# One adaLN transformer block on one core: moving the last modulation row out of the start, re-filling TensorE's waits there, and running one projection by column halves

## The chip, the cores and the metric

The kernel runs on one core of a Trainium2 chip. A core has a matmul engine (TensorE, PE in the profile, with its weight loads as PEld), a vector engine (DVE), a scalar engine (ACT), a general engine (POOL) and a queue engine (SP), which work side by side and wait for each other by semaphores, and 16 DMA engines that move data between HBM and on-chip memory. The metric is device time in microseconds (us) of one execution, taken as the median of several.

## The reference, cut to what matters

One sequence of 2048 tokens, width D = 576, 32 heads of 18, hidden width F = 4608. Everything is bfloat16.

```
mod = silu(c) @ w_mod                         # one row of 6*576: sa, ca, ga, sb, cb, gb
h = layernorm(x) * (1 + ca) + sa
q, k, v = h @ wqkv                            # per head, scale 18**-0.5
o[s] = softmax over 8 keys (s, s-2, ... s-14) of q[s].k, times v
x = x + ga * (o @ wo)
h = layernorm(x) * (1 + cb) + sb
x = x + gb * (((h @ w_gate) * (h @ w_up)) @ w_down)
```

So `ga` is needed when the first attention output is projected, and `gb` only when the first `w_down` product is written out.

## The kernel before, in words

The tokens go through in ten chunks (`SIZES`: four of 128, then six of 256). Each chunk has a first half, `project` (layer norm, a transposition of the rows, modulation by `sa`/`ca`, then q, k and v), and a second half, `attend` (logits from products of q with shifted k, softmax, weighted sum of shifted v, projection by `wo`, residual, second layer norm, transposition, modulation by `sb`/`cb`). The gated matmuls of a chunk are `gate_up`; `down` multiplies by `w_down` for 512 tokens at a time. There are seven passes over the gate/up weights: chunks 0, 1, 2 and 3 alone (passes 0 to 3, 128 tokens each), and then pairs of 256-token chunks. In pass p the matmuls of `gate_up` are interleaved with `attend` of the next chunk(s) and `project` of the one after; a `Pacer` releases these pieces when the pass has reached a set share of its length. The shares are the tables `AT_SHORT`, `AT_FIRST` and `AT`: `wo0=.59, v0=.66` means that the `wo` projection is issued at 59% of a pass and v at 66%. In passes 0 to 3 a scheduler orders the instructions on every engine; from pass 4 on TensorE's order is as written.

Everything before pass 0 is the prologue (lines 783 to 824): its order on all engines is as written by hand, as a list of `next(...)` and `go(..., label)` on three generators, `a0 = project(0)`, `a1 = project(1)` and `b0 = attend(0)`. `warm(n)` (L275) issues n matmuls on zeros whose result nobody reads. In the order of TensorE the prologue is:

- `warm`, the columns of `sa`/`ca` (L245, four 32-column groups of the array side by side), the transposition of chunk 0 (L414), `warm(9)`;
- q and k of chunk 0 (L485, forty matmuls `pq`), their last 64 columns (L492, five matmuls `pr` against a packed copy `wqr`), `warm(5)`, the transposition of chunk 1;
- logits of chunk 0 (L553, `lgT`), with the ten matmuls of the `ga` row (L264) between their two halves; the columns of `sb`/`cb` (L245);
- v of chunk 0 (L510, `pv`, ten matmuls), which waits for the weights `wv`; the shifted softmax weights (`up`, L587); v of chunk 1 (L510);
- the weighted sum (L603, `oTs`), `wo` of chunk 0 (L628, ten matmuls into the two banks of one tile `pw`, halves alternating), q and k of chunk 1 (L485), the ten matmuls of the `gb` row (L264), the transposition for the second layer norm (L414), and then `pgu` (L672), the first matmul of pass 0.

On DVE the projection is followed by two multiplications by `ga` (L633), one addition (L634), statistics in two halves (L377) and their merging (L378); ACT computes the reciprocal deviation (L383, L384); DVE normalises (L395); after the transposition ACT and DVE modulate (L434, L436). ACT copies the two row results into `ga_bc` and `gb_bc` (L268, L269).

Loads are put in queues by three engines. POOL's queue holds, in order: `wmB` (the `sb`/`cb` columns), `wv`, `wo`, the `gb` columns of `w_mod` (two DMAs, 576 KB and 72 KB, into the free half of `wmC`), the v rows of chunks 0 and 1 to HBM (L517), the gate/up weights of blocks 0 to 2 (`load_early`, L284), the shifted reads of v (`vsh`, L527), and blocks 3 to 6. SP's queue holds `c`, the `sa`/`ca` and `ga` columns, q/k weights, x, and the short weight tails `gr`; at the end of pass 0 (L340 to L346, after its next-to-last block) it gets x of chunks 4 and 5, part of `w_down`, and then two blocks of weights for pass 1, each held until DVE has written one element behind the hidden values of that block.

PSUM, where TensorE writes, is divided into two pools: `att` (two banks) and `mlp` (three tiles of two banks). `banks2` and `bank` choose between them. The v projection of a chunk (`pvA`, `pvB`) takes the two `att` banks that `wo` (`pwA`, `pwB`) had just before.

## Time and profile before

| | |
|---|---|
| runs | 5: median 578.23 us, 576.76 to 580.79 |
| profiled execution | 578.34 us, of which 576.6 us are the span from first to last instruction |
| TensorE busy | 563.8 us, 98% of the span |
| DVE, ACT, POOL busy | 318.5, 221.4 and 95.6 us |
| granted TensorE clock | 0.997 on average; below 1 in one stretch near 24 to 27 us |
| HBM read, written | 70.93 MB, 8.67 MB |

TensorE is busy nearly all the time, so the time moves when work is added to or taken from it, or when one of its few waits changes. Nearly all its idle time lies in the first 40 us, so the prologue is read from the timeline of each engine, instruction by instruction; behind it the passes are read from the waits.

### The profile page before, as it was taken

To read this page: it belongs to the slowest core of one execution; us is meant where nothing else is said; L and a number is where in the kernel's file an instruction comes from. 1 tells how busy PE (TensorE), PEld (TensorE's weight loads), DVE (VectorE), ACT (ScalarE), POOL (GpSimd) and SP (SyncE) were. 2 spreads that over 40 slices of the span, in tenths; PEclk is the share of its full clock that TensorE was granted. 3 is DMA by queue.
4 is the path that set the end of the run, shared out by engine and by line. 5 is a ranking of instruction groups with operands and counts; after the bars stand their busy time and mean duration, and the time that the engine had idled before them with its cause. 6 is when DMAs were issued, how large, how long until landed. Compare 5 with 4: busy or idle time off the path is not lost.

```text
span 576.6 us, 12231 instructions
## 1 busy us (share of the span) xinstructions
PE 563.8 (98%) x5167; PEld 369.7 (64%) x5171; DVE 318.5 (55%) x695; ACT 221.4 (38%) x386; POOL 95.6 (17%) x165
## 2 busy tenths in 40 slices
PE   8799999999999999999999999999999999999996
PEld 3468898888878764554468764554457744444775
DVE  5578696868778775655484635754384422122101
ACT  3446655655602225445442005454440035454200
POOL 4373202020113212020601240011200200000000
PEclk9899999999999999999999999999999999999999
DMA  9999774349760444477302633486202224450000
GB/s 287 264 333 339 262 228 142 119 159 337 231 202 25 147 128 148 121 220 230 96 1 77 218 91 106 128 242 215 80 0 57 68 64 126 150 164 1 1 22 20
DMA packets 68457, 84.32 MB, mean 146 GB/s; under 512 B 19618, under 2 KB 59506, under 8 KB 68402
## 3 DMA queue, kind: packets, MB, share of 16 engines
q1 hardware_dynamic: 56738, 45.86, 27.1%
q0 software_dynamic: 9104, 34.44, 18.0%
q10 hardware_dynamic: 2560, 3.25, 1.7%
q8 instruction: 40, 0.66, 0.5%
q14 instruction: 15, 0.12, 0.1%
HBM read 70.93 MB, written 8.67 MB: 138 GB/s over the span
## 4 chain that ended last, share of the span: by engine, by line
PE 85%; DMA 7%; DVE 3%; ACT 2%; POOL 1%; issue 1%; SPq 0%; ACTq 0%; POOLq 0%; DVEq 0%
PE pgu L672 41%; PE acc L720 24%; PE pgu L681 6%; PE pq L485 5%; DMA wd<-in_B_w_up_dram 4%; PE lgT L553 2%; DMA wv<-in_A_wqkv_dram 2%; DMA wqk<-in_A_wqkv_dram 2%; PE pwB L628 2%; PE pwA L628 1%; PE pvB L510 1%; PE pvA L510 1%; DVE ln_stats L377 1%; PE pr L492 1%; ACT gu L689 0%
## 5 line engine op out<-in xcount | busy, mean ns | idle before, releaser
L672 PE MATMUL pgu<-h2T,gm 128*128 128x512 bf16 (+1 forms) x1504 | 238.5, 311 | 1.1 <-ACT gu L689 0.7
L689 ACT CAST gu<-pgu 128x1024 bf16<-128x1024 f32 (+1 forms) x180 | 145.4, 844 | 141.5 <-PE pgu L681 115.3
L672 PEld LDWEIGHTS <-gm 128*128 128x128 bf16 x1504 | 118.4, 98 | 108.1 <-issue 16.3
L720 PE MATMUL acc<-wd,hh 128*128 128x288 bf16 x1152 | 146.5, 286 | 0.5 <-DVE y L726 0.5
L690 DVE TENSOR_TENSOR hh<-gu 128x512 bf16<-128x512 bf16 (+1 forms) x180 | 66.1, 372 | 128.1 <-ACT gu L689 126.9
L720 PEld LDWEIGHTS <-hh 128*128 128x128 bf16 x1152 | 112.3, 98 | 29.5 <-issue 1.2
L544 DVE TENSOR_TENSOR prod<-qT,kT 128x1280 bf16<-128x1280 bf16 (+1 forms) x80 | 46.7, 633 | 14.4 <-PE lgT L553 13.2
L527 POOL DMA_DIRECT2D vsh<-vd x30 | 22.6, 758 | 153.0 <-DMA vd<-v_sb 88.9
L729 POOL DMA_DIRECT2D out_dram<-y x15 | 8.4, 563 | 215.8 <-DVE y L728 215.8
L485 PE MATMUL pq<-hT,wqk 128*128 128x256 bf16 (+1 forms) x400 | 41.2, 251 | 0.9 <-DMA wqk<-in_A_wqkv_dram 0.9
L726 DVE TENSOR_TENSOR y<-acc,gb_bc 128x576 bf16<-128x576 f32 (+1 forms) x17 | 12.2, 720 | 52.3 <-PE acc L720 52.3
L611 DVE TENSOR_TENSOR vsh<-vsh,attn 128x2304 bf16<-128x2304 bf16 x30 | 39.9, 1354 | 0.2
L681 PE MATMUL pgu<-h2T,gr 64*128 64x512 bf16 (+1 forms) x376 | 37.0, 311 | 0.0
L485 PEld LDWEIGHTS <-wqk 128*128 128x128 bf16 x400 | 32.3, 98 | 6.9 <-DMA wqk<-in_A_wqkv_dram 1.6
L672 PE MATMUL pgu<-h2T,wd 128*128 128x128 bf16 x512 | 34.5, 219 | 0.0
L383 ACT ACTIVATE ln_rstd<-ln_stats,eps 128x2 f32<-128x2 f32 (+1 forms) x20 | 5.9, 296 | 67.2 <-DVE ln_stats L378 67.1
L672 PEld LDWEIGHTS <-wd 128*128 128x128 bf16 x512 | 30.2, 98 | 1.3 <-DMA wd<-in_B_w_up_dram 0.2
L377 DVE BATCH_NORM_STATS2 ln_stats<-x_t 128x6 f32<-128x288 bf16 x64 | 26.2, 447 | 1.9 <-DMA x_t<-in_A_x_dram 1.3
L681 PEld LDWEIGHTS <-gr 64*128 64x128 bf16 x376 | 12.2, 94 | 18.9 <-issue 11.5
L425 POOL TENSOR_SCALAR h2T<-h2T,modc 128x256 bf16<-128x256 bf16 x25 | 15.8, 637 | 29.8 <-DMA h2T<-xn_d 29.8
L510 PEld LDWEIGHTS <-hT 128*128 128x128 bf16 x160 | 15.8, 101 | 7.4 <-issue 2.2
L612 DVE TENSOR_TENSOR vsh<-vsh 128x2304 bf16<-128x2304 bf16 x15 | 20.3, 1354 | 0.0
(147 smaller groups left out, 449.5 us busy)
## 6 DMA issues: line engine op xcount, KB each, us to landing
vsh<-vd POOLq DMA_DIRECT2D x30, 576.0 KB, 6.0
gm<-in_B_w_gate_dram SPq DMA_DIRECT2D x24, 512.0 KB, 3.8
gm<-in_B_w_up_dram SPq DMA_DIRECT2D x24, 512.0 KB, 5.2
wd<-in_B_w_down_dram SPq DMA_DIRECT2D x4, 1152.0 KB, 7.6
gm<-in_B_w_gate_dram POOLq DMA_DIRECT2D x5, 512.0 KB, 12.1
gm<-in_B_w_up_dram POOLq DMA_DIRECT2D x5, 512.0 KB, 12.2
out_dram<-y POOLq DMA_DIRECT2D x15, 144.0 KB, 2.1
wd<-in_B_w_gate_dram POOLq DMA_DIRECT2D x4, 512.0 KB, 10.3
```

The costliest lines, as they stand in the source:

```text
L377: nc.vector.bn_stats(stats[:, j, hf, :], src[j][:, hf * 288:(hf + 1) * 288])
L485: nc.tensor.matmul(pq[:, gi, 0:C], lhsT=wqk[:, kt, w0:w0 + P], rhs=h[:, kt, :], start=(kt == 0), stop=(kt == KT - 1))
L510: nc.tensor.matmul(pv[q][:, 0:288], lhsT=h[:, kt, j * P:(j + 1) * P], rhs=wv[:, kt, q * 288:(q + 1) * 288], start=(kt == 0), stop=(kt == K ...
L527: nc.gpsimd.dma_start(vsh[:].rearrange("p w d h -> p w (d h)"), src)
L544: nc.vector.tensor_tensor(prod[:, 0:nm, 0:C], qT[:, 0:nm, 0:C], kT[:, 0:nm, off:off + C], ALU.mult)
L611: nc.vector.tensor_tensor(vsh[:], vsh[:], attn[:, j, ws, None, :].to_broadcast([P, WG, DH, H]), ALU.mult)
L612: nc.vector.tensor_tensor(va[:], va[:], vb[:], ALU.add)
L672: nc.tensor.matmul(by_half(out[:, t, n, 0:C]), lhsT=gu_blocks[b][0][:, kt, t, (i + n) * P:(i + n + 1) * P], rhs=tokens(slice(0, P), kt), s ...
L681: nc.tensor.matmul(by_half(out[:, t, n, 0:C]), lhsT=gu_blocks[b][1][rows, (i + n) * P:(i + n + 1) * P], rhs=tokens(rows, KT - 1), start=(f ...
L689: nc.scalar.copy(g, ps[u][:, :, :, 0:C].rearrange("p t n c -> p n t c"))
L690: nc.vector.tensor_tensor(hh[:, fs, cs], g[:, :, 0, :], g[:, :, 1, :], ALU.mult)
L720: nc.tensor.matmul(acc[:, q, 0:288], lhsT=hh[:, f, j * P:(j + 1) * P], rhs=wd[:, f, q * 288:(q + 1) * 288], start=(f == 0), stop=(f == FT ...
```

## The change

It does five things.

1. The `gb` row leaves the prologue. Its weights are no longer loaded on POOL's queue; `load_gb` loads them on SP's queue at the end of pass 0, behind x of chunks 4 and 5 and ahead of the part of `w_down`, into one `vsh` tile and one `y` tile, with a one-element DVE copy ahead of each. `gb_row` computes the row in pass 1, between `wo` of chunk 2 (0.59 of the pass) and v of chunk 3 (0.66): forty matmuls of 288 columns, four 32-column groups side by side, into the two `att` banks, then two ACT copies of 128x288 into `gb_bc`. `sc32` moves to a pool that stays allocated.
2. The ten matmuls of the `ga` row move from between the logits to the place of `warm(5)`, ahead of the transposition of chunk 1; their two ACT copies go ahead of the logits' copy.
3. q of chunk 1 (twenty matmuls) moves ahead of v of chunk 0; k of chunk 1 stays behind `wo` of chunk 0. A `warm(5)` stands behind it where the `gb` row was.
4. In chunk 0 the last 64 columns of q and k are computed between q and k, by ten matmuls of 64 columns straight from `wqk`.
5. `wo` is computed by column halves (five matmuls for A, then five for B) in every chunk. In chunk 0 addition and statistics also go by halves: multiply, add, statistics of A, then of B; and the result goes to two `att` banks.

In the order that the scheduler makes of pass 1, ACT has the two copies into `gb_bc` behind both instructions of the reciprocal deviation of chunk 2, and ahead of the third copy of gate/up results; before, v of chunk 3 was next there.

```diff
-AT_SHORT = dict(AT_FIRST, qkr=.47, ws=.51, oT=.52, wo0=.59, v0=.66, v1=.72, h2T=.80)
+AT_SHORT = dict(AT_FIRST, qkr=.47, ws=.51, oT=.52, wo0=.59, gb=.63, v0=.66, v1=.72, h2T=.80)
...
+    def load_gb(behind):
+        rows["gb"] = vshp.tile([P, WG, DH, H], BF, name="vsh")[:].rearrange("p w d h -> p w (d h)"), outp.tile([P, D], BF, name="y")
+        main, rest = rows["gb"]
+        nc.vector.tensor_copy(main[0:1, 0, 0:1], behind)
+        nc.vector.tensor_copy(rest[0:1, 0:1], behind)
+        nc.sync.dma_start(main, w_mod[0:(KT - 1) * P, 5 * D:6 * D].rearrange("(k p) n -> p k n", p=P))
+        nc.sync.dma_start(rest[0:64], w_mod[(KT - 1) * P:D, 5 * D:6 * D])
+
+    def gb_row():
+        main, rest = rows["gb"]
+        pg = banks2(False, F32, "pg")
+        for kt in range(KT):
+            for q in range(2):
+                qs = slice(q * 288, (q + 1) * 288)
+                for g in range(4):
+                    nc.tensor.matmul(pg[q][32 * g:32 * (g + 1), 0:288], lhsT=sc32[kp(kt), kt, :], rhs=main[:, kt, qs] if kt < KT - 1 else rest[0:64, qs],
+                                     start=(kt == 0), stop=(kt == KT - 1), skip_group_check=True)
+        for q in range(2):
+            nc.scalar.copy(gb_bc[:, q * 288:(q + 1) * 288], pg[q][:, 0:288])
...
             for cx in (4, 5):
                 load_x(cx, nc.sync, behind=late["hh"][0:1, b * FB, 0:1])
+            load_gb(late["hh"][0:1, b * FB, 0:1])
...
-            load_rows(nc.gpsimd, wmC[:, :, D:2 * D], w_mod[:, 5 * D:6 * D])
...
-                pq = bank(ci == 1, "pq").rearrange("p (g c) -> p g c", g=2)
+                pq = bank(ci == 1 and t == 1, "pq").rearrange("p (g c) -> p g c", g=2)
...
-            pr = bank(ci == 1, "pr")
+            pr = bank(ci < 2, "pr")
             for kt in range(KT):
-                nc.tensor.matmul(pr[:, 0:C], lhsT=wqr[:, kt, :], rhs=h[:, kt, :], start=(kt == 0), stop=(kt == KT - 1))
+                if ci == 0:
+                    for t in range(2):
+                        nc.tensor.matmul(pr[64 * t:64 * (t + 1), 0:C], lhsT=wqk[:, kt, t * D + 512:(t + 1) * D], rhs=h[:, kt, :],
+                                         start=(kt == 0), stop=(kt == KT - 1), skip_group_check=True)
+                else:
+                    nc.tensor.matmul(pr[:, 0:C], lhsT=wqr[:, kt, :], rhs=h[:, kt, :], start=(kt == 0), stop=(kt == KT - 1))
...
-        for part in (v, qk) if ci == 1 else (qk, v):
-            yield from part()
+        for nm in qk():
+            if ci == 1 and nm == "k0":
+                yield from v()
+            yield nm
+        if ci == 3:
+            yield "gb"
+            gb_row()
+        if ci != 1:
+            yield from v()
...
-            pw = banks2(ci == 0, F32, "pw")
-            for m in range(KT):
-                for q in range(2):
+            pw = banks2(False, F32, "pw")
+            for q in range(2):
+                for m in range(KT):
                     nc.tensor.matmul(pw[q][:, 0:288], lhsT=oT[:, m, j * P:(j + 1) * P], rhs=wo[:, m, q * 288:(q + 1) * 288],
...
                 nc.vector.tensor_tensor(y[:, qs], pw[q][:, 0:288], ga_bc[:, qs], ALU.mult)
-            nc.vector.tensor_tensor(x_t[j][:], y[:], x_t[j][:], ALU.add)
+                if by_half:
+                    nc.vector.tensor_tensor(x_t[j][:, qs], y[:, qs], x_t[j][:, qs], ALU.add)
+                    ln_half(tiles, x_t, j, q)
+            if not by_half:
+                nc.vector.tensor_tensor(x_t[j][:], y[:], x_t[j][:], ALU.add)
...
-        go(a0, "qkr")
+        go(a0, "k1")
         next(a1)
         next(a0)
-        warm(5)
-        go(a1, "v0")
+        ga_row_mm()
+        go(a1, "q0")
         for _ in range(3):
             next(b0)
-        mod_row_mm(wmC, 0)
+        ga_row_copy()
         go(b0, "up")
-        mod_row_copy(0, ga_bc)
         pick = mod_pick(mod_columns(wmB, 0))
+        go(a1, "v0")
         next(a0, None)
...
         go(a1, "qkr")
-        next(b0)
-        mod_row_mm(wmC, 1)
+        warm(5)
         go(b0, None)
         go(a1, None)
-        mod_row_copy(1, gb_bc)
```

## The prediction, made before the changed kernel had run

> **What bounds the kernel now.** I read the page first, then TensorE's waits, then the granted clock in stretches of 1 us, then each engine's timeline in the first 45 us and around 80 to 92 us.
>
> ```profile
> span 576.6 us, 12231 instructions
> PE 563.8 (98%) x5167; PEld 369.7 (64%) x5171; DVE 318.5 (55%) x695; ACT 221.4 (38%) x386; POOL 95.6 (17%) x165
> PEclk9899999999999999999999999999999999999999
> ```
>
> TensorE is busy for 563.8 of 576.6 us. Work taken off another engine is worth nothing unless TensorE waits for it. The clock row shows one slice below full speed, the second (14 to 29 us). TensorE's two costliest waits for something that the change touches are (total, times, longest):
>
> ```profile
> PE pv L510 <- DMA wv<-in_A_wqkv_dram: 2.1, 1, 2.1
> ...
> PE pgu L672 <- ACT gu L689: 0.7, 2, 0.4
> ```
>
> The first is in the prologue: v of chunk 0 waits for its weights. The stretches around it (busy time of PE, weight loads, DVE, ACT, POOL, then granted clock, DMA share, GB/s) show what that wait brings:
>
> ```profile
> 22.00:23.00 1.00, 0.52 (x24) 0.28 (x17) 0.49 (x2) 0.45 (x2) 0.00 (x0) 1.00 1.08 194
> ...
> 24.00:25.00 1.00, 0.42 (x2) 0.25 (x2) 0.83 (x2) 0.00 (x0) 0.00 (x0) 0.52 1.03 218
> 25.00:26.00 1.00, 1.00 (x6) 0.64 (x5) 0.00 (x0) 0.00 (x0) 0.00 (x0) 0.50 1.06 184
> ...
> 27.00:28.00 1.00, 1.00 (x15) 0.81 (x14) 0.51 (x2) 0.70 (x2) 0.00 (x0) 0.77 1.16 283
> ```
>
> From about 24.05 to 27.46 us the clock is half, just when those ten matmuls run. TensorE's own timeline (start, length, what):
>
> ```profile
> 24.58 2.56 PE L510 MATMUL pv<-wv,hT 128*128 128x288 bf16 x10 [2.06 <-DMA wv<-in_A_wqkv_dram]
> ...
> 32.13 1.40 PE L628 MATMUL pw<-wo,oT 128*128 128x288 bf16 x10 [0.33 <-DVE oT L621]
> ...
> 36.17 1.13 PE L264 MATMUL pr<-wm,sc_bc 128*128 128x512 bf16 x4 [0.16 <-issue]
> 37.25 0.34 PE L414 MATMUL turnA<-identw,o_sb 128*128 128x128 bf16 x3
> ...
> 38.59 1.86 PE L672 MATMUL pgu<-h2T,gm 128*128 128x128 bf16 x24 [0.32 <-ACT h2T L436]
> ```
>
> From the landing of `wv` (24.58) to the first matmul of pass 0 (38.59), a chain through all engines sets the end. Behind it only DMA is close: the chain of waits runs through two weight loads,
>
> ```profile
> 33.02 9.10 DMA wd<-in_B_w_up_dram
> 42.41 13.28 DMA wd<-in_B_w_up_dram
> ```
>
> and the second, block 5 of pass 0, lands at 55.69, just as its weights are wanted (the weight load waits 0.22 us). At the place in pass 1 where the `gb` row goes, ACT's order matters:
>
> ```profile
> 86.13 0.58 ACT L689 CAST gu<-pgu 128x512 bf16<-128x512 f32 x1 [0.19 <-PE pgu L672]
> 87.28 0.29 ACT L383 ACTIVATE ln_rstd<-ln_stats,eps 128x1 f32<-128x1 f32 x1 [0.56 <-DVE ln_stats L378]
> 87.60 0.20 ACT L384 ACTIVATE ln_rstd<-ln_rstd 128x1 f32<-128x1 f32 x1
> 87.71 0.38 ACT L514 CAST v_sb<-pvA 128x288 bf16<-128x288 f32 x1
> ```
>
> **Before the landing of wv: nothing.** The `ga` row took 1.71 us (18.67 to 20.38). In the place of `warm(5)` (15.48 on) it ends near 17.1, so the transposition of chunk 1, at 16.94 before, starts 0.1 to 0.2 later. Its weights are issued at 7.3 and 7.7 and land near 14.6, so it doesn't wait. Where it was it hid DVE's eight products (3.04 us); without it TensorE waits for those. The ten 64-column matmuls replace five of 128 columns (0.44 us) and let DVE start the products about 0.7 earlier (16.0 for 16.68). ACT's order is then the bound: five modulations to 19.3, `ga` copies (0.7), logits' copy at 20.0 for 20.89. So the `sb`/`cb` columns end near 21.6 instead of 22.5; chunk 1's q (twenty matmuls, half of the forty in 2.40, so 1.2) fills up to 22.8. All of it ends before 24.58, so the sum is zero whatever these are between 0 and 1.7 us. The wait shrinks only to 1.7.
>
> **The clock in v of chunk 0: -1.2, or 0.** At half clock these ten matmuls hold TensorE from 24.58 to 26.93, 2.35. The same ten in pass 0 go from 59.08 to 60.30, 1.22. With 0.1 for the `up` matmuls behind, a full clock is worth 1.2, and the whole chain shifts: ACT's copies of v, the stores and block loads queued behind them on POOL, DVE's weighted sum. Will the clock stay? The half clock lasted 3.41 us and began after a stretch of 3.41 in which TensorE was busy about 47% (1.88 minus a wait of 0.26 of 3.41); the stretch from 10.4 to 13.8, busy 73%, cost none. With q of chunk 1 filled in, the same stretch holds the columns (0.99) and q (1.2), about 64%. That lies nearer to 73, so I take -1.2; 0 stays as the other end. The Trainium skill's page "TensorE: Matmul & The Clock Gate", section "Why this matters for your kernels", warns only of idle gaps above about 3 us, and says in its Part 1 that the windows are free-running. Taken alone, that rule would keep the clock with a gap of 1.7, giving the 578.2 below; but this trace halved after a gap of 2.06, so the rule is too lenient here and 579.4 has to stay open.
>
> **From wo to pass 0: -0.75.** Before, DVE's first multiplication starts 1.43 after `wo` does (33.56), and multiplications, addition, statistics and merging end at 35.98; ACT, busy with casts, starts the reciprocal deviation at 36.20. By halves, A is out after five matmuls (0.62 and 0.17 to arrive), so DVE starts at 0.8. It then works 0.41 + 0.26 (half an addition of 0.46, with its fixed part) + 0.41, twice, and 0.21: 2.4, and ends near 35.35. ACT has only k's two casts left by then. Between 0.6 (DVE's own gain) and 0.85 (ACT waiting for nothing) I take 0.75. TensorE's `gb` row (1.54 us) and 1.2 of q leave this stretch and 1.1 of warming comes in, but the deviation is later than either, so they count nothing.
>
> **Pass 0's weight stream: 0.** A gain of 1.95 is kept only if block 5 comes earlier too. The `gb` weights (0.66 MB, issued 20.52 and 21.37, landing about 10 us later, near 31) shared the engines at a DMA share above 1 up to then, ahead of blocks 0 to 5 on POOL's queue. Freed at the 345 GB/s of the stretches after 40 us they are worth 1.9 us. The block loads are issued 4 to 13 us before they land, so issue doesn't pace them. Kept gain: 1.9; ends 0.2 and 1.95.
>
> **Pass 1: +1.8.** The forty matmuls of `gb_row` are of the kind of L245: four start within 10 ns and the next four 110 ns later at 256 columns; all forty took 0.99. With 288 columns ten rounds of 124 ns make 1.24. Ends: 0.99, and 4.9 if nothing overlaps (40 x 0.122, the start-to-start of `pv`). They need both banks of `wo`: A is multiplied near 84.5, B near 85.1, the row starts at 85.4, so no wait. But `pvA`, wanted at 85.89 + 1.24 = 87.13, now needs `pgA` copied, and ACT has this copy behind the deviation of chunk 2, which waits for DVE's statistics (87.1 by the same rows). Copies then run 87.55 to 87.95 and to 88.25 (0.38 each): TensorE stands about 0.85 for A and 0.15 more for B, so 1.0, between 0 (if DVE is early) and 1.5. Behind that, a wait that exists now goes: TensorE waited at 91.22 (0.44) for gate/up results that ACT copied late, held up by the deviation of chunk 3 until 90.40. That deviation comes no later (DVE's statistics for it keep their time), while the gate/up results come about 2 later. 1.24 + 1.0 - 0.44 = 1.8.
>
> The two loads on SP push `w_down` and two blocks by 1.9 us of DMA time and 1 us of issues (0.4 and 0.6 like the others). The DMA share is full from 68 to 82 and 0.10 after, and block 1, whose tails land at 80.5, is first used at 89.2: hidden, with 6 us left. The row's own weights land near 77. Two one-element DVE copies (0.13 each) and the shift in `vsh` buffers (the one that chunk 3 takes is free at 81.2, its load is issued at 92.5) are covered likewise. `wo` by halves in later chunks: TensorE never waited for DVE there, so 0; the waits behind 92 us total 1.4, so no more than 0.5 either way.
>
> **Sum.** -1.9 + 1.8 = -0.1 against the profiled execution's 578.34 (576.6 and 1.7 around it), which is 0.1 above the median of 578.23: 578.2.
>
> **Rivals.**
> - *Half clock stays.* For it: the wait is still 1.7. Against: more work in the window. The 1.2 is lost: 579.4.
> - *The weights of pass 0 come no earlier,* so the prologue's gain becomes a wait at blocks 3 and 5 and the change doesn't do what it is set up for. For it: block 3 landed at 48.75 and was used at 48.94. Against: 1.9 us of DMA work is gone ahead of them. 578.34 + 1.8 = 580.1.
> - *The gb row doesn't overlap its four groups* (slower). One place, pass 1: 4.9 instead of 1.24, so 581.8. It passes the half per cent from 106 ns per matmul on. L245 speaks against it, with 25 ns.
> - *ACT is not late in pass 1.* Statistics of chunk 2 come a microsecond earlier: 577.2. DVE's rows speak against it.
>
> **How the numbers follow.** The likeliest case 0.47 (own range 577.0 to 579.4), half clock 0.24, no earlier weights 0.11, no overlap 0.06, no ACT wait 0.12. About 2.9 us, half a per cent, is what a measurement of this kernel can tell from no change. Faster than 575.3 needs the last case and a favourable run, 0.07 with what I have not seen; slower than 581.1 is the no-overlap case, a part of the no-earlier-weights case and the unseen, 0.13; the rest, 0.80, is within. With the spread of the five runs around the outer cases the range is 576.0 to 581.0.
>
> **What would show it.** Right: a granted clock of 1.00 during `pv` of chunk 0, `pgu` first near 36.7, a wait of about 1 us at `pvA` in pass 1 released by ACT, `gb_row` 1.2 to 1.3 long, no new wait for weights. Wrong: half clock at 24 to 27; waits for `wd` in 45 to 56; `pgA`/`pgB` 100 ns apart.

## The result, and the profile after

The changed kernel takes 579.39 us (median of 38 runs, 577.28 to 581.84) and the kernel before 577.61 (65 runs, 576.23 to 580.96): a ratio of 1.0029 with a 95% interval of 1.0021 to 1.0037. That is 1.8 us slower. It lies within the half per cent that the prediction called no change and within its range, but the interval excludes 1, and the prediction's sum had -0.1. So 1.9 us of loss were not in the sum. The profiled execution of the changed kernel took 579.12 us.

From its page (first lines, and the row of the granted clock):

```profile
span 577.4 us, 12313 instructions
PE 562.4 (97%) x5203; PEld 369.1 (64%) x5206; DVE 320.2 (55%) x698; ACT 222.1 (38%) x386; POOL 93.8 (16%) x163
PEclk9999999999999999999999999999999999999999
```

TensorE is busy 1.4 us less than before (1.2 of it because the ten matmuls of `pv` no longer run at half clock), and yet the span is 0.8 longer: the time went into waits, not into work. The clock is full throughout. TensorE's waits name where (total, times, longest):

```profile
PE pgu L730 <- DMA wd<-in_B_w_up_dram: 1.5, 2, 0.8
...
PE turnA L446 <- ACT v_sb L559: 1.2, 1, 1.2
PE turnA L446 <- DVE o_sb L427: 1.2, 1, 1.2
...
PE pv L555 <- DMA wv<-in_A_wqkv_dram: 0.5, 1, 0.5
...
PE pvA L555 <- ACT gb_bc L291: 0.3, 1, 0.3
```

The wait for `wv` went from 2.1 to 0.5. Four of these waits are not in the list of the kernel before: 1.5 us for the `up` weights in pass 0 (before, only a weight load waited there, for 0.22), 1.2 for ACT's copy of v in pass 2, 1.2 for `o_sb` in the prologue, where the matmuls of the `gb` row had stood, and 0.3 for ACT's copy of `gb` in pass 1.

TensorE's timeline in the prologue (start, length, what) answers the rows shown of before:

```profile
22.57 1.39 PE L555 MATMUL pv<-wv,hT 128*128 128x288 bf16 x10 [0.51 <-DMA wv<-in_A_wqkv_dram]
...
28.94 0.79 PE L682 MATMUL pwA<-wo,oT 128*128 128x288 bf16 x5 [0.33 <-DVE oT L673]
...
33.74 0.34 PE L446 MATMUL turnA<-identw,o_sb 128*128 128x128 bf16 x3 [1.21 <-DVE o_sb L427]
...
34.78 1.69 PE L730 MATMUL pgu<-h2T,gm 128*128 128x128 bf16 x24 [0.30 <-ACT h2T L468]
```

Pass 0 starts at 34.78 instead of 38.59, a gain of 3.8 where the prediction had 1.95. Then the gain is lost in four places. The table follows single matmuls of the gate/up and down products through both traces. Its last columns use a second profile of the unchanged kernel (run `before_again`, below), which turned out to be the more ordinary one:

| start of | before, first profile | after | difference | before, second profile | difference |
|---|---|---|---|---|---|
| pass 0 (`pgu` 0) | 38.59 | 34.78 | -3.8 | 35.16 | -0.4 |
| pass 1 (behind the waits for `up` weights) | 67.08 | 64.72 | -2.4 | 65.09 | -0.4 |
| pass 1 behind the `gb` row and v of chunk 3 | 89.44 | 89.24 | -0.2 | 87.44 | +1.8 |
| pass 1, 5 us on | 94.45 | 93.65 | -0.8 | 92.46 | +1.2 |
| pass 2 behind the transposition at 121.8 | 123.69 | 124.00 | +0.3 | 121.71 | +2.3 |
| last instruction's end | 576.6 | 577.40 | +0.8 | 575.30 | +2.1 |

The waits of pass 0, as the prediction's second rival had them and as it had named them for a sign of being wrong (start, length, idle time before):

```profile
46.14 0.40 PE L730 MATMUL pgu<-h2T,wd 128*128 128x128 bf16 x4 [0.85 <-DMA wd<-in_B_w_up_dram]
53.41 0.84 PE L730 MATMUL pgu<-h2T,wd 128*128 128x128 bf16 x12 [0.66 <-DMA wd<-in_B_w_up_dram]
```

They are blocks 3 and 5. In pass 1 the `gb` row starts at 83.17, each four groups 0.12 us behind the last, and this is its end and what follows:

```profile
84.39 0.29 PE L288 MATMUL pgB<-y,sc 64*32 64x288 bf16 x4
84.62 0.62 PE L730 MATMUL pgu<-h2T,wd 128*128 128x128 bf16 x8
85.51 0.28 PE L555 MATMUL pvA<-wv,hT 128*128 128x288 bf16 x1 [0.28 <-ACT gb_bc L291]
85.81 0.28 PE L555 MATMUL pvB<-wv,hT 128*128 128x288 bf16 x1
```

The row takes 1.45 us (83.17 to 84.62). Then `pvA` stands until ACT has emptied its bank. The fourth loss is in pass 2, and the prediction did not speak of it. ACT's timeline there:

```profile
117.85 0.35 ACTq L562 DMA_DIRECT2D vd<-v_sb  x1
...
121.37 0.40 ACT L559 CAST v_sb<-pvA 128x288 bf16<-128x288 f32 x1 [1.00 <-DMA vd<-v_sb]
```

Chunk 4 has 256 tokens, so its v is copied and stored in two halves through the same tile `v_sb`. ACT's copy of the second half waits until the first half is stored (3.44 us from issue to landing, 1.76 in the kernel before), and TensorE, whose next transposition needs the `att` banks that ACT is to empty, waits behind it:

```profile
121.82 0.33 PE L446 MATMUL turnA<-identw,o_sb 128*128 128x128 bf16 x3 [1.24 <-ACT v_sb L559]
```

In the kernel before, the same store landed at 120.41. ACT's copy of the second half started at 121.08 without waiting for it, so the room was 0.67 us, and the transposition came 0.13 behind TensorE's work ahead of it:

```profile
118.65 0.34 ACTq L517 DMA_DIRECT2D vd<-v_sb  x1
...
121.08 0.38 ACT L514 CAST v_sb<-pvA 128x288 bf16<-128x288 f32 x1
```

```profile
121.51 0.33 PE L414 MATMUL turnA<-identw,o_sb 128*128 128x128 bf16 x3
```

Why the same 144 KB take nearly twice as long is seen in the view of the DMA traffic from 117.8 to 121.4 us (40 slices of 0.09 us; then the queues):

```profile
DMA  0000000000988984000000001000010000000000
...
q10 hardware_dynamic: 144, 0.15, 12.7%
q8 instruction: 1, 0.02, 2.1%
...
vd<-v_sb ACTq DMA_DIRECT2D x1, 144.0 KB, 3.4
```

Nothing else moves in this stretch. The store's 144 packets are done within 0.6 us on fifteen DMA engines (the block of 8s and 9s). On one engine stands a packet of another queue: 16 KB of instructions, from 118.79 to 120.00 (1.22 us). The store's nine packets on that engine finish only at 120.76, in the thin traffic to the right. The page counts 40 such packets in the whole span, in the kernel before too, for some 10,400 instructions of TensorE, one for about every 256 of them:

```profile
q8 instruction: 40, 0.66, 0.5%
```

So where one falls should depend on how many instructions TensorE has gone through. The program before has 10,344 TensorE instructions (matmuls and weight loads; its profile records 10,338), the changed one 10,414 (10,409 recorded), that is 70 more: thirty more matmuls for the `gb` row and five of warming in its old place, two instructions each. In the kernel before the loads nearest to this store came at 112.6 and 122.7 us. The one at 122.7 started when 3,517 of TensorE's recorded instructions had started, the one at 118.79 in the changed kernel after 3,504, and in a kernel with 64 instructions more (`more_instructions`, below) the same one came at 115.6, after 3,500. So it is the count that places it, and the added instructions brought it forward onto the store.

The Trainium skill's page "DMA: Bandwidth & Descriptors", section "Queues, rings and completion order", says that a DMA engine takes turns between its queues a whole packet at a time. The rows above agree: the store's packets on one engine stood behind a packet of 1.2 us.

### The profile page after: what moved, and what is told of

Its sections match the earlier page's. It is cut to its first block, busy times and chain, and to the rows that moved or that the text cites. A ratio compares the mean times of both kernels' runs of the same rounds, so it can differ in the third digit from the quotient of the medians.

```text
span 577.4 us, 12313 instructions
## 1 busy us (share of the span) xinstructions
PE 562.4 (97%) x5203; PEld 369.1 (64%) x5206; DVE 320.2 (55%) x698; ACT 222.1 (38%) x386; POOL 93.8 (16%) x163
## 4 chain that ended last, share of the span: by engine, by line
PE 86%; DMA 8%; DVE 2%; ACT 1%; POOL 1%; issue 1%; SPq 0%; ACTq 0%; POOLq 0%; DVEq 0%
PE pgu L730 41%; PE acc L778 24%; PE pgu L739 6%; PE pq L519 5%; DMA wd<-in_B_w_up_dram 4%; PE lgT L605 2%; DMA wv<-in_A_wqkv_dram 2%; DMA wqk<-in_A_wqkv_dram 2%; PE pwA L682 2%; PE pwB L682 1%; PE pvA L555 1%; PE pvB L555 1%; PE pr L537 1%; DMA vd<-v_sb 1%; ACT gu L747 0%
## 5 line engine op out<-in xcount | busy, mean ns | idle before, releaser
L747 ACT CAST gu<-pgu 128x1024 bf16<-128x1024 f32 (+1 forms) x180 | 145.5, 844 | 143.4 <-PE pgu L739 122.7
L579 POOL DMA_DIRECT2D vsh<-vd x30 | 22.5, 754 | 155.8 <-DMA vd<-v_sb 144.0
L687 DVE TENSOR_TENSOR y<-pwA,ga_bc 128x288 bf16<-128x288 f32 x16 | 7.3, 455 | 23.1 <-PE pwA L682 23.1
```

The source lines that it names most:

```text
L579: nc.gpsimd.dma_start(vsh[:].rearrange("p w d h -> p w (d h)"), src)
L747: nc.scalar.copy(g, ps[u][:, :, :, 0:C].rearrange("p t n c -> p n t c"))
```

## The experiments

Three explanations were to be told apart. (a) The expected gains of the prologue were never there to be won: the first profile of before had a late landing of `wv` and half clock that are not the kernel's rule. (b) Pass 0's weight stream takes back what the prologue wins. (c) The added TensorE instructions push an instruction load onto a store that TensorE waits for. Against (c) stands the plain rival that the `gb` row's own work in pass 1 makes the loss. In the expectations, which stand here as they were recorded, (a) is theory D, (b) is theory F, and (c) is theory A, from `after_again` on theory I.

### One part undone, one part alone

`no_gb_move` is the changed kernel without part 1; `gb_move_alone` is the kernel before with part 1 only.

```diff
 # no_gb_move, against the changed kernel
...
-            load_gb(late["hh"][0:1, b * FB, 0:1])
...
+            load_rows(nc.gpsimd, wmC[:, :, D:2 * D], w_mod[:, 5 * D:6 * D])
...
-        if ci == 3:
-            yield "gb"
-            gb_row()
...
-        warm(5)
+        next(b0)
+        gb_row_mm()
         go(b0, None)
         go(a1, None)
+        gb_row_copy()
```

```diff
 # gb_move_alone, against the kernel before
...
+            load_gb(late["hh"][0:1, b * FB, 0:1])
...
-            load_rows(nc.gpsimd, wmC[:, :, D:2 * D], w_mod[:, 5 * D:6 * D])
...
+            if ci == 3 and part is v:
+                yield "gb"
+                gb_row()
...
-        mod_row_mm(wmC, 1)
+        warm(5)
         go(b0, None)
         go(a1, None)
-        mod_row_copy(1, gb_bc)
```

> The change with its first part undone: the gb weights are loaded in the prologue and the gb row is computed there, as before; parts 2 to 5 stay. Theory A (PE's instruction loads): the late waits of the changed kernel, 1.2 us for chunk 4's v store in pass 2 and 0.6 near 158 us, come from the 70 added PE instructions, which move PE's 16 KB instruction loads against the stores of v; this kernel has as many PE instructions as the one before (10344), so both waits are at most 0.3 us. The gb weights compete again, so wv lands 1.3 to 2 us later than in the changed kernel (24 to 24.5), pgu starts at 36 to 37, and blocks 3 and 5 of pass 0 then hold TensorE for about 2 us: the total is 0 to 0.5 us below the kernel before. Rival B (the order in the head moves the stores): the late waits are there here too, and the total is 1 us or more above the kernel before.

> The kernel before with the first part of the change alone: gb weights loaded at the end of pass 0, gb row in pass 1 by forty matmuls, a warm(5) in the prologue where the row was. PE has 10414 instructions, and the v projections of chunk 4 stand at the same places of PE's program as in the changed kernel. Theory A: the wait of about 1.2 us at the transposition in pass 2 and the longer one near 158 us are there as in the changed kernel, wv lands 1.3 to 2 us earlier than before, pass 1 costs 1.6, and the total is 0.5 to 1.5 us above the kernel before. Rival B: no such waits in passes 2 and 3, total between 1 us below and 0.3 above. Rival C (wv lands earlier because of the new order in the head, not because the gb weights have gone): wv lands at 24.5 and the total is 2.5 us or more above the kernel before.

Measured: 577.59 (ratio 0.999, 0.998 to 1.0001) without part 1, and 580.34 (1.004, 1.0026 to 1.0054) with part 1 alone; the kernel before on the same chip took 577.75. So part 1 makes the loss, and the other four parts change nothing that these runs can tell. Part 1 alone costs 2.6 us, more than the 0.5 to 1.5 expected. In the profile of `no_gb_move` the store in pass 2 took 1.79 us and TensorE waited 0.12 behind it. `wv` landed at 22.75 there, where 24 to 24.5 was expected: a first sign that the late landing was an accident of one execution. In `gb_move_alone` the store took 3.97 and the wait was 1.78, and the half clock came behind it (columns as in the prediction's windows: busy time of PE, weight loads, DVE, ACT, POOL, then the granted clock):

```profile
122.00:123.00 1.00, 0.35 (x4) 0.25 (x4) 0.00 (x0) 0.70 (x2) 0.35 (x1) 1.00 0.00 0
...
124.00:125.00 1.00, 1.00 (x13) 1.00 (x13) 1.00 (x5) 1.00 (x4) 0.76 (x1) 0.63 0.81 233
125.00:126.00 1.00, 1.00 (x13) 1.00 (x11) 0.47 (x2) 0.56 (x2) 0.60 (x1) 0.50 0.99 207
126.00:127.00 1.00, 1.00 (x12) 0.97 (x10) 0.00 (x0) 0.00 (x0) 0.89 (x2) 0.50 0.88 327
```

From 124.27 to 127.68 (3.41 us) the clock is half, and this cost another 1.6 us in that execution: over this stretch the gate/up matmuls fall behind those of the changed kernel by that much. The Trainium skill's page "TensorE: Matmul & The Clock Gate", in "Why this matters for your kernels", warns of idle gaps above about 3 us. This gap was 1.78 and sufficed; the 1.24 and 1.56 in the two profiles of the changed kernel did not.

### The gb row by ten matmuls, and the same kernel with still more instructions

If the number of instructions decides where a packet falls, fewer of them and more of them must both cure it. `gb_by_ten` computes the row by ten matmuls with a broadcast weight (10,354 instructions). `more_instructions` leaves the row alone and replaces the five warming matmuls behind k of chunk 1 by 37 small ones that take the same 1 us (10,478).

```diff
 # gb_by_ten, against the changed kernel
-                for g in range(4):
-                    nc.tensor.matmul(pg[q][32 * g:32 * (g + 1), 0:288], lhsT=sc32[kp(kt), kt, :], ...
+                n = P if kt < KT - 1 else 64
+                nc.tensor.matmul(pg[q][:, 0:288], lhsT=sc32[kp(kt), kt, 0:1].to_broadcast([n, P]), ...
```

```diff
 # more_instructions, against the changed kernel
+    def warm_small(n):
+        pw = ps_mlp.tile([P, 2, 512], F32, name="warm", tag="mlp")
+        for _ in range(n):
+            nc.tensor.matmul(pw[:, 0, 0:64], lhsT=zeros[:, 0:P], rhs=zeros[:, 0:64], start=True, stop=True)
...
-        warm(5)
+        warm_small(37)
```

> The changed kernel with the gb row in pass 1 by ten matmuls with 128 weight columns (a broadcast of the same column) instead of forty with 32: 60 PE instructions fewer (10354), nothing else moved. Theory A: TensorE's instruction load falls about 64 instructions behind chunk 4's second v projection, so its store is not delayed: the wait at the transposition in pass 2 is below 0.3 instead of 1.24, the one near 158 about 0.2; with 0.2 for the ten matmuls (1.22 for 1.45) the time is 1.3 to 2 us below the changed kernel, about equal to the kernel before or 0.5 below. Rival B (the waits come from the times of loads and copies, whatever the count): both waits stay and the time is within 0.4 us of the changed kernel.

> The changed kernel with the last warm(5) of the prologue made of 37 matmuls of 64 columns instead of 5 of 512: 64 PE instructions more (10478), about 2 us of PE time in a place where TensorE idles 1.2 us behind 1.1 of warming, so no more than 0.1 on the path. Theory A: the instruction load in pass 2 now falls between chunk 4's first v projection and its store, so the store is not delayed: the wait at the transposition is below 0.4 instead of 1.24 and the time 0.7 to 1.7 us below the changed kernel. Rival B: same as the changed kernel within 0.4 us, or slower.

Measured: 578.37 (1.0015, 1.0004 to 1.0027) and 577.99 (1.000, 0.9988 to 1.0012), before 577.75. In both profiles the store took 1.79 us and the wait in pass 2 was 0.13. `more_instructions` is the telling one: it does everything that the changed kernel does, and 64 instructions more, and is 1.4 us faster. The DMA view around the same store (117.4 to 119.3 us), with no instruction packet in it:

```profile
DMA  0000000000000000000489999979631000000000
...
q10 hardware_dynamic: 144, 0.15, 22.9%
...
vd<-v_sb ACTq DMA_DIRECT2D x1, 144.0 KB, 1.8
```

Two parts of the expectations missed. `gb_by_ten` came out 1.0 us below the changed kernel, where 1.3 to 2 were expected, and its interval still lies above 1. And another wait, 0.56 us at `wo` near 157 us behind a v store in pass 3, had first seemed to be the change's, and was to go as well; it stayed in both. The next run shows that the kernel before has it too. Ten matmuls take 1.43 us (83.51 to 84.94 us), so the forty in four groups gain nothing for sixty more instructions.

### The kernel before, a second time, and with 70 more instructions

```diff
 # before_plus70, against the kernel before (before_again is the kernel before itself)
...
         next(a0)
-        warm(5)
+        warm_small(40)
         go(a1, "v0")
```

> The kernel before, unchanged, profiled once more. The three kernels with either the gb move or the new order of the head, but not both, all show wv landing at 22.7 to 23.1 us, although one still loads the gb weights in the prologue and one has the head's old order. Theory D: the late landing (24.5), the wait of 2.06 and the half clock in the first profile of the kernel before belong to that execution, not to the kernel: here wv lands at 22.5 to 23.2, the wait is at most 1 us, the clock stays full, pgu starts at 35.5 to 36.3, and the ratio is 1.000 within 0.0012. Rival E: the wait of 2 us and the half clock are the kernel's own: wv lands after 24 and pgu starts near 38.5.

> The kernel before with nothing changed but the warm(5) ahead of chunk 1's transposition, made of 40 matmuls of 64 columns instead of 5 of 512: 70 PE instructions more (10414, as in the changed kernel), at a place ahead of the wait for wv. Theory A (instruction loads against the v store): chunk 4's first v store in pass 2 lands 3 us or more after its issue instead of 1.8, TensorE waits 1.1 to 1.8 at the transposition behind it instead of 0.13, and the time is 1.2 to 2.5 above the kernel before. Rival B: no such wait, same time within 0.4 us.

Measured: 577.37 (1.0002, 0.9993 to 1.0012) and 578.79 (1.0029, 1.0018 to 1.004), before 577.36. Seventy instructions without any work in them cost 1.4 us, most of what the whole change costs. The profile of `before_plus70` has a store of 3.34 us with a wait of 1.15 in pass 2, and besides a wait of 1.48 for `wv` with half clock behind it; against `before_again` 0.6 us of that prologue is left at the start of pass 1, and pass 2 adds 1.0.

The second profile of the kernel before speaks for (a). TensorE's waits and the same stretch of the clock:

```profile
PE pv L510 <- DMA wv<-in_A_wqkv_dram: 1.1, 1, 1.1
PE pgu L672 <- DMA wd<-in_B_w_up_dram: 1.0, 3, 0.6
```

```profile
22.00:23.00 1.00, 0.38 (x4) 0.30 (x4) 0.94 (x2) 0.59 (x2) 0.00 (x0) 1.00 1.13 214
...
24.00:25.00 1.00, 1.00 (x17) 0.82 (x13) 0.65 (x2) 0.70 (x2) 0.00 (x0) 1.00 1.11 240
25.00:26.00 1.00, 0.84 (x12) 0.51 (x10) 1.00 (x2) 0.54 (x2) 0.96 (x2) 1.00 1.15 236
```

`wv` lands at 22.6, the wait is 1.1 instead of 2.1, the clock is full and pass 0 starts at 35.16 instead of 38.59. The kernel before was already where the prediction wanted to bring it. And its pass 0 already waits 1.0 for `up` weights. Two profiles alone would not say which is the rule. But each execution has a mean clock on record: the four profiles with a stretch of half clock in them have 0.996 or 0.997, the fourteen others 0.998 or more, and of 146 executions of the kernel before, timed beside the experiments, 124 have 0.998 or more.

### Pass 0 without part of its weight stream

`light_stream` is the changed kernel without the `up` weights of blocks 3, 4 and 5 in passes 0 to 3: they are not loaded there, and the `gate` weights are multiplied in their place, so that only these loads are left out and TensorE's work is the same.

```diff
-        for t in range(2):
+        for t in range(1 if b in (3, 4, 5) else 2):
             load_gm(gu_blocks[b][0], b, t, nc.gpsimd)
...
-  lhsT=gu_blocks[b][0][:, kt, t, ...
+  lhsT=gu_blocks[b][0][:, kt, 0 if pi < KEPT_PASSES and b in (3, 4, 5) else t, ...
```

> The changed kernel without the up weights of blocks 3, 4 and 5 in passes 0 to 3 (three loads of 512 KB left out of pass 0's stream; the matmuls use the gate weights in their place, so the numbers computed for these blocks are not the reference's). Theory F (pass 0's weight stream takes back the head's gain): the two waits of TensorE for these blocks in pass 0, 0.85 and 0.66 us, are gone, pass 1 starts 1.5 to 1.9 us sooner against the start of pass 0 than in the changed kernel, and the time is 1.2 to 1.9 us below it. Rival G (the head's gain is lost elsewhere): pass 1 starts no sooner, same time within 0.4 us.

Measured: 577.95 (1.0014, 0.9996 to 1.0032), before 577.36. No wait for weights is left in its pass 0, which takes 28.17 us from its first gate/up matmul to that of pass 1, where the changed kernel's takes 29.94. So (b) holds, by one profile each: 1.8 us of pass 0 is the weight stream's, and with this stream a prologue that ends earlier is not worth its full time. The time does not fix the price of the waits to better than 1 us, since the median fell by 1.4 with a wide interval, and the profile of this run also had no slow store in pass 2 (1.84 us).

### The change again, and the row undone but its instructions kept

`no_gb_plus70` is `no_gb_move` with five of the nine warming matmuls ahead of q of chunk 0 replaced by forty small ones, that is with the instruction count of the changed kernel and none of its pass 1.

```diff
 # no_gb_plus70, against no_gb_move (after_again is the changed kernel itself)
...
-        warm(9)
+        warm(4)
+        warm_small(40)
```

> The changed kernel itself, a second time. Theory I (instruction loads): the wait of about 1.2 us at the transposition near 121.8 us of pass 2, behind a v store of 3.4 us, is tied to the number of TensorE instructions and so comes again (0.9 to 1.8 us), where an accident of one execution would leave it at 0.13. Some of its executions run at half clock for about 3.4 us, so the mean granted clock falls below 0.9985 in about a third of them. Time 579.2 to 579.6, 1.5 to 2.0 above the kernel before. Rival C (chance): no such wait, and 577.8 to 578.4.

> The changed kernel with the gb row and its weights back in the prologue, and five of its warming matmuls there (512 columns) replaced by forty of 64 columns in the same time: the 70 TensorE instructions that the moved row adds are there, the row's work in pass 1 isn't. Theory I (instruction loads): the v store of pass 2 meets an instruction load again, the wait near 121 us is 0.9 to 1.8 us instead of 0.12, and the time is 578.6 to 579.2, 1.0 to 1.6 above the same kernel without these instructions (577.6). Rival R (the row's own work in pass 1 makes the loss): the wait stays at 0.13 and the time at 577.4 to 577.9.

Measured: 579.18 (1.0031, 1.0018 to 1.0044) and 579.23 (1.003, 1.0019 to 1.0042), before 577.5. The wait came again in the second profile of the changed kernel, 1.56 us behind a store of 3.76. And the kernel without the row in pass 1, but with the instructions, is as slow as the change. The time is as (c) has it, but the one profile of `no_gb_plus70` was not: its store met the load only at its end and took 1.83, the wait in pass 2 was absent, and its loss of that execution came from the prologue instead:

```profile
PE pv L571 <- DMA wv<-in_A_wqkv_dram: 2.8, 1, 2.8
```

`wv` landed at 25.15, and half clock followed. So the count alone was shown to cost the time, but not yet where. In part it is the half clock: six of its twelve executions have a mean clock of 0.996 or 0.997, with a median of 580.4, and the six others 578.4.

### A second tile for the store

The direct test takes away what makes ACT wait, and nothing else: the second half of v goes through a `y` tile instead of `v_sb`, in chunk 4 only (`..._two`). Order and number of instructions stay the same on every engine.

```diff
-                vt = v0 if ci == 0 else v_sb
+                vt = v0 if ci == 0 else outp.tile([P, D], BF, name="y") if ci == 4 and j == 1 else v_sb
```

> The changed kernel with one line changed: the second half of chunk 4's v is copied into a y tile, so that ACT's copy no longer waits for the store of the first half. Instruction count and the order on every engine are the same. Theory I (the v store of pass 2 meets an instruction load and TensorE stands behind it): the store may be as slow as before, but the wait at the transposition near 121.8 us falls from 1.2 to 1.6 to at most 0.2, executions at half clock get rarer, and the time is 577.8 to 578.3, 1.0 to 1.4 below the changed kernel (579.2 to 579.4). Rival E (that wait is one symptom; the time is lost elsewhere): 578.9 to 579.4 although the wait is gone.

> The kernel with the gb row back in the prologue and 70 more TensorE instructions (579.23), with the same line changed. Its one profile had no wait in pass 2, but a late wv landing (25.15) and half clock behind it. Theory I: other executions did wait in pass 2, and the time falls to 577.7 to 578.3. Rival E (its loss sits in the prologue): 578.9 to 579.4.

> The kernel with the gb row back in the prologue, without the extra instructions (577.59), with the same line changed: the candidate for the fastest version. Its wait in pass 2 was 0.12 us, so both theories expect no change beyond 0.2: 577.3 to 577.7, a ratio to the kernel before of 0.998 to 1.000.

Measured, before 577.54: 577.61 (1.0006, 0.9996 to 1.0016), 578.26 (1.0011, 0.9998 to 1.0025) and 577.00 (0.9989, 0.9981 to 0.9998). One line gives back 1.6 of the 1.8 us that the change lost; the first and the third came out 0.2 and 0.3 below what was expected. In the profile of `no_gb_plus70_two` the collision happens and nobody waits for it: the store is issued at 116.72 and lands at 120.56 (3.84 us, an instruction packet of 1.39 in it), while ACT goes on at 119.14 and TensorE at 119.57:

```profile
116.72 0.34 ACTq L578 DMA_DIRECT2D vd<-v_sb  x1
...
119.14 0.38 ACT L575 CAST y<-pvA 128x288 bf16<-128x288 f32 x1
```

```profile
119.57 0.33 PE L461 MATMUL turnA<-identw,o_sb 128*128 128x128 bf16 x3
```

(The profile of `after_two` itself had no collision, with a store of 1.79, so that its wait is gone proves nothing; the time does.) `no_gb_plus70_two` stays 1.26 above the kernel without the extra instructions. Its profile says where: TensorE waits behind a v store in pass 3, where chunk 5 still goes through one tile (store 149.66 to 154.90):

```profile
155.43 0.49 PE L461 MATMUL turnA<-identw,o_sb 128*128 128x128 bf16 x6 [1.07 <-ACT v_sb L575]
```

What made this store slow is not shown: an instruction packet starts 2.0 us behind its issue, but 0.8 MB of other loads move beside it, and in the other profiles this store, with 0.4 to 0.8 MB beside it, takes 2.8 to 4.2.

### A second tile in every chunk from 4 on

```diff
-                vt = v0 if ci == 0 else v_sb
+                vt = v0 if ci == 0 else outp.tile([P, D], BF, name="y") if ci >= 4 and j == 1 else v_sb
```

> The changed kernel with the second half of v in a y tile in every chunk from 4 on. Theory I (v stores that meet instruction loads, wherever they fall): the wait of 0.52 for the gate/up copy at the first down matmul near 156 us, behind a store of 3.9, falls to 0.2 or less; 577.1 to 577.6, at or up to 0.5 below the version with chunk 4 alone (577.61). Rival N (instructions cost as such): no change from 577.61, and 1 us above the last kernel of this call.

> The gb row in the prologue, 70 more TensorE instructions, second half of v in a y tile in every chunk from 4 on. Theory I: its waits in pass 3 (1.07 at a transposition and 0.62 at the first down matmul, behind a store of 5.2) go, and it comes to 576.9 to 577.5, at most 0.6 above the same kernel without the extra instructions. Rival N: it stays at 578.0 to 578.5, 1.2 above.

> The gb row in the prologue, no extra instructions, second half of v in a y tile in every chunk from 4 on. Theory I: 576.6 to 577.0 (577.00 with chunk 4 alone, whose profile still has waits of 0.22 and 0.19 behind v stores): a ratio to the kernel before of 0.998 to 0.999. Rival N: the same, so this run only sets the level from which the extra instructions are counted.

> The kernel before with the second half of v in a y tile in every chunk from 4 on. Theory I: it gains what the other kernels gain without extra instructions, 577.56 to about 576.0 to 576.5 (no_gb_move lost 1.7 by the same edit), so the change by itself is worth between +0.2 and +0.8 (its pass 1 costs more than its prologue saves). Rival G: the change is a gain in itself, and this kernel stands above 576.9. If stores never mattered in the kernel before, it stays at 577.3 to 577.7.

Measured (before 577.56 for the first three, 577.46 for the last):

| kernel | TensorE instructions | one tile | two tiles from chunk 4 on | ratio to the kernel before, two tiles |
|---|---|---|---|---|
| before | 10,344 | 577.46 | 576.66 | 0.9988 (0.9979 to 0.9996) |
| changed | 10,414 | 579.18 | 576.74 | 0.9986 (0.997 to 1.0001) |
| parts 2 to 5 | 10,344 | 577.59 | 575.87 | 0.9973 (0.9962 to 0.9983) |
| parts 2 to 5 and 70 instructions | 10,414 | 579.23 | 576.04 | 0.9982 (0.9971 to 0.9992) |

With one tile, 70 instructions cost 1.6 us (579.23 against 577.59). With two they cost 0.2, and the intervals of the two ratios overlap. So the instructions cost nothing as such that these runs can tell; what they cost is the store that ACT and TensorE wait for. The first three expectations held in direction and were too careful in size: 576.74 for 577.1 to 577.6, 576.04 for 576.9 to 577.5, 575.87 for 576.6 to 577.0. The wait of 0.56 near 157, which every profile of a kernel with one tile there had, but for the first one of the kernel before, is gone as well, and in the changed kernel the first store of v in the next pass follows that of this pass 1.2 us sooner. The last expectation missed on the other side: the kernel before gained 0.8, not 1.1 to 1.5, so the change by itself comes to +0.1. The intervals of the two ratios (0.9979 to 0.9996 and 0.997 to 1.0001) overlap so far that its sign is open.

The slow store and the instruction packet go together in all profiles. Of the eighteen profiled executions of these kernels, seven had a store of chunk 4's first half of 3.3 to 4.0 us, and each of the seven had an instruction packet starting 0.9 to 1.5 us behind the issue. The eleven others took 1.76 to 1.84; eight had no such packet, and three had one that started 1.4 to 1.5 behind the issue, the late edge at which it went either way. No other load or store was under way beside this one in any of them, but for the first packets of the next v store in one.

`no_gb_two_all` (575.87) is the fastest version: the `gb` row left where it was, parts 2 to 5 kept, and a second tile for v. It beats the kernel before by 0.27% and the changed one by 0.6%.

## Why the prediction came out as it did, step by step

**Before the landing of wv, nothing:** right in that the moved rows cost nothing, wrong in the wait that it left. 1.7 us was to remain; 0.51 did, because `wv` landed at 22.5 and not at 24.5. This landing is not the change's doing: the unchanged kernel had it at 22.6 the second time.

**The clock in v of chunk 0, -1.2:** this step failed. The clock was full, as forecast, but in the kernel before it is full in its second profile too. The term was read from a single execution that was out of the ordinary (2.06 of wait, half clock, +3.4 at the start of pass 0, of which 1.3 was left at the end). Against the second profile the whole prologue gives 0.4, not 1.95. The warning was there: that execution had a mean clock of 0.997, and a second profile of the kernel before would have shown it. The mechanism was sound and its size too: from the start of `pv` to that of `wo` it took 7.55 us before and 6.37 after, so 1.18 less than in that execution. What failed is that the term took this execution for the kernel.

**From wo to pass 0, -0.75:** 6.46 us became 5.84, so -0.62 against the first profile, and -0.33 against the second (6.17). Right sort, slightly large. The wait at the transposition (1.21) shows that the chain through DVE and ACT still sets the end there, as argued.

**Pass 0's weight stream, 0:** the mechanism was right, the claim that it would keep up was half right. Of 3.8 us gained against the first profile, 1.4 were given back in waits at blocks 3 and 5, the place named by the rival. Taking the `gb` weights out of the stream is worth something: at the start of pass 1 the changed kernel is 0.4 ahead of the second profile of before, `no_gb_move` 0.75 behind it. That is 1.1 for the 1.9 estimated, seen in one pair of profiles.

**Pass 1, +1.8:** right within 0.2, by one profile each. The row took 1.45 for 1.24 (a pause of 0.1 ahead of the last two fours, whose data lie in the other tile, is part of it), the waits at `pvA` and `pvB` 0.28 and 0.2 for 1.0, and the wait that was to go at 91 went, with 0.6 for 0.44. In all 2.17 were lost and 0.6 won, net 1.57. ACT was late, but by less: its copies start 1.91 behind the row's start for 2.15, and `pvA` is wanted 2.06 behind it for 1.73.

**"The waits behind 92 us total 1.4, so no more than 0.5 either way":** this is the step that made the forecast wrong in sign. The waits that existed were counted, and the stores that could turn into waits were not. The store of chunk 4 had no wait behind it in the profile of before (0.13) because it took 1.76; it had 0.67 us of room, and an instruction packet that seventy instructions brought forward onto it added 1.7, of which ACT waited 1.00. In the changed kernel's two profiles TensorE waited 1.24 and 1.56 there, and the second tile gave 1.6 back. No rival had it.

**The sum.** With the store's wait taken out of both kernels, the change comes to +0.1 us (576.74 against 576.66) where the sum had -0.1. The four other parts are worth -0.8 there (575.87 against 576.66; the intervals of the ratios just overlap), and moving the `gb` row +0.9. So what the sum weighed nearly balanced, but from partly wrong terms, which is luck, and what it did not weigh cost 1.6 to 1.8.

**The half clock.** It was seen behind waits of 1.48, 2.06 and 2.77 in the prologue and of 1.78 in pass 2, but not behind two of 1.6 in the prologue, so the length of a wait alone does not decide. The prediction had judged it by how much of a stretch of 3.41 us TensorE is busy, and the traces bear that out. Cut into such stretches, counted from the changes of the clock in each of the eighteen profiles, every one in which TensorE was busy for 40% or less was followed by half clock, and none with 54% or more was; between 42 and 49% two of six were, both in the prologue. The stretch ahead of v of chunk 0 was busy for 48% in the first profile of the kernel before and for 78% in the changed kernel, where the prediction had 47 and 64. The half clock is also a part of the change's loss: of its 39 recorded executions 12 have a mean clock of 0.996 or 0.997, with a median of 580.7, and the 27 others 578.9, while the 124 of the kernel before without it have 577.5. So by this mark about 1.4 of the 1.8 us stay without half clock, and it adds the rest; where in these executions it falls is not on record. None of the eleven executions of `after_two` has it.

**Left open.** Why `wv` lands between 22.0 and 23.6 in fifteen of the eighteen profiles and between 24.5 and 25.2 in three was not tried.

## What to carry to other kernels

Ask of every wait that a profile does not show how much room it has: a copy that waits for the store of the same tile is one slow store away from the engine that bounds the kernel, and a second tile removes the risk (here 0.8 to 3.2 us for one line, depending on the kernel). Count instructions as well as their time: adding or removing instructions that take no time shifts every later instruction load, and an unrelated place may pay; before such a change is called a loss, shift the count by some tens of empty instructions and measure again. And profile the kernel before twice before a gain is read from a stall at its start.

## What the runs showed of the hardware that was not expected

TensorE's instructions arrive during the execution, 16 KB for about 256 of them, in a packet that holds one DMA engine for 0.9 to 2.0 us. A store of 144 KB, spread over sixteen engines and with no other load beside it, took 3.3 to 4.0 us with such a packet at its start and 1.8 without. Forty matmuls in four column groups took as long as ten that use the whole array (1.45 and 1.43 us at 288 columns). And the clock halved for 3.41 us behind an idle gap of 1.78, once in pass 2, where TensorE had been busy for 40% of the 3.41 us before.
